# A recurrent attention with a two-layer projection on one core: the product with the state in four small tiles, more buffers for r and k, and a wait for GpSimd

## The chip, the cores and the metric

The kernel runs on one core of a Trainium2 chip. A core has TensorE (PE, matrix products; its weight loads are listed as PEld), VectorE (DVE), ScalarE (ACT), GpSimd (POOL), and SyncE (SP), which issues the DMA transfers here. They run side by side, each in the order of its own queue, and wait for each other by semaphores. The metric is the device time of one execution in microseconds; a time shown is the median of several runs.

## The reference

Inputs: `r`, `k`, `v` of shape (4, 8, 768, 48) (batch, heads, tokens, head width), a decay `w` and a bonus `u` per head and channel, and two weight matrices of 384 x 2048 and 2048 x 384 with a slope `alpha`. For each batch and head a 48 x 48 state runs over the tokens:

```python
for t in range(S):
    cur = np.einsum('bhd,bhe->bhde', u[None] * kt, vt)
    y[:, :, t] = np.einsum('bhd,bhde->bhe', rt, state + cur)
    state = w[None, :, :, None] * state + np.einsum('bhd,bhe->bhde', kt, vt)
# x = y as (3072, 384)
h = x @ w_in
g = np.maximum(h, 0.0) + alpha * np.minimum(h, 0.0)
out = g @ w_out
```

## The kernel before, in words

**Attention.** The 768 tokens are cut in six chunks of 128 (`C = 6`, `L = 128`). A unit, `attention(c, q, at)`, is one chunk `c` and one pair of heads `q` (0 to 3) for all four batches. Head 0 of the pair lies on partitions 0 to 47, head 1 on 64 to 111 (`half(g)`). With r and k scaled by powers of the decay (DVE, L302), a unit makes the scores k r in PSUM (`scores`, L342: 8 fp32 matmuls, 48 rows deep, on the two halves of the array's rows), lays them by a mask over a diagonal that holds the bonus term (ACT L349, DVE L353), and then `out` sums in the PSUM tile `y` two products: the state `T[q]` with r (L363) and v with the masked scores (L368). `state_product` makes k v (L380) into the PSUM tile `U`; DVE adds it to the decayed state (L445), one instruction for each head. An fp32 matmul is two instructions on PE, so four matmuls are eight in the trace.

`T[q]` is 112 x 4 x 112: the two heads' 48 x 48 states stand on the diagonal of each 112 x 112 block, the rest is zero (POOL memsets, L205), so one matmul of 112 rows and 112 columns serves both heads. The state of chunk 0 is copied by ACT (L440), the last chunk makes none. The bonus term of chunks 0 and 1 comes from a small matmul (L317), that of chunks 2 to 5 from POOL: r k (L327), times u (L329), then a DVE reduce (L333). `y` is split in a rounded part `xh` (ACT L410) and a rest `xl` (DVE L412), each one instruction of 112 x 512; head pair 0's rows are then copied to their places by small DMAs (`lower`).

**Projection.** A step is one chunk and one of 16 weight tiles: `m_in` (L458, 9 matmuls of 512 columns into `hp`), the activation (ACT L464, DVE L465, ACT L468, DVE L469) and, three steps later, `m_out` (L489, 9 matmuls into `acc`). 96 steps: tiles 0 to 8 for chunks 0 and 1, then tiles 9 to 15 for both, then chunks 2 to 5 with all 16. A weight tile comes by one DMA and is decoded once (`weights`: ACT L248, DVE L250, L252, L255, ACT L258 for `wh`, DVE L259 for `wl`).

**Order.** Nothing is ordered by hand. Each piece of work is handed to a planner (`Plan.add`) with its engine, an assumed duration, the buffers it reads and writes, and a rank. `in_order` simulates the engines as a list scheduler: among the pieces that are ready on an engine, the one of lowest rank goes next. The program is emitted in that order, so durations, ranks, buffer counts and dependencies all move the instructions of every engine. Buffers of one name rotate: a piece of the n-th user waits for all pieces of the (n - bufs)-th. r and k use `raw` (4 buffers); chunk 0's third pair borrows `o`, its fourth `wx`, the scratch of the weights' decode. `rr` (r for POOL) has 2 buffers, `kk` 3. In PSUM, the scores use `A0` and `A1`, `U` takes `A0` behind the scores, `y` has one bank.

Of the kernel before, what the change touches and what calls it, by code (L numbers as in the profile page):

```python
# [14 lines left out]
ALU = mybir.AluOpType  # L15
# [116 lines left out]
def rwkv_prelu_kernel(ctx: ExitStack, tc, rk, vkr, wP, uP, u, wall, alpha, w, r_all, k_all, v_all, oT):  # L132
# [41 lines left out]
    def half(h):  # L174
        return slice(HI * (h % 2), HI * (h % 2) + D)
# [100 lines left out]
    def attention(c, q, at):  # L276
        first, last = c == 0, c == C - 1

        r, k0 = (sb([112, B, L], *(("o", 2) if q == 2 else ("wx", 2)) if first and q > 1 else ("raw", 4))
                 for _ in range(2))  # L280
        v, k = sb([128, 2 * B, D], "v", 4), sb([128, 2 * B, D], "kk", 3)
        n = 2 * B * D
# [25 lines left out]
        if c < 2:  # L308
            prod = sb([112, B, L], "g", 3)
            add("DVE", 0.7, lambda: nc.vector.tensor_tensor(out=prod(), in0=r(), in1=k0(), op=ALU.mult),  # L310
                r=[r, k0], w=[prod], rank=10 * q - 88 if first else at - 3)
            sums, cols = (pb([128, 2 * B], "y"), slice(0, 8)) if c else (bank, slice(8 * q, 8 * q + 8))
            mine = sums if c else (sums, q)

            def c_sum():
                for b in range(B):
                    nc.tensor.matmul(sums()[:, cols][:, 2 * b:2 * b + 2], prod()[:, b], uw()[:, q], start=True,  # L317
                                     stop=True, skip_group_check=True)

            add("PE", 1.0, c_sum, r=[prod, uw], w=[mine], rank=at - 0.2 - 40 * first - 20 * (c == 1))  # L320
            add("ACT", 0.2, lambda: nc.scalar.activation(cu(), sums()[:, cols].rearrange("p (b g) -> p g b", g=2), AF.Copy), r=[mine],
                w=[cu], rank=at - 1)
        else:
            rt = sb([128, 2 * B, D], "rr", 2)
            load(rt, lambda: nc.sync.dma_start(rt().rearrange("p x e -> p (x e)"), vkr[c, q, :, 2 * n:]), 192,
                 early + 0.1 * q + 0.2, [wh[0]])
            add("POOL", 1.2, lambda: nc.gpsimd.tensor_tensor(out=rt(), in0=rt(), in1=k(), op=ALU.mult), r=[k], w=[rt],  # L327
                rank=at - 2)
            add("POOL", 1.2, lambda: nc.gpsimd.tensor_tensor(  # L329
                out=rt().rearrange("p (g b) e -> p g b e", g=2), in0=rt().rearrange("p (g b) e -> p g b e", g=2),  # L330
                in1=utab()[:, 2 * q:2 * q + 2, None, :].broadcast_to([128, 2, B, D]), op=ALU.mult),
                r=[utab], w=[rt], rank=at - 2)
            add("DVE", 0.55, lambda: nc.vector.tensor_reduce(  # L333
                out=cu().rearrange("p g b -> p (g b)"), in_=rt(), axis=AX.X, op=ALU.add), r=[rt], w=[cu], rank=at - 1.8)
# [20 lines left out]
                rank=10 * q - 76 + g if first else at - 1.5 if c != 1 else -60)  # L355


        y = pb([112, B, L], "y" if not first or q % 2 == 0 else "hp", 1 if not first or q % 2 == 0 else 2)

        def out():  # L360
            if not first:
                for b in range(B):
                    nc.tensor.matmul(y()[:, b], T[q]()[:, b], r()[:, b], start=(b == 0), stop=False,  # L363
                                     skip_group_check=True)
            for b in range(B):
                for g in range(2):
                    rows, x = (slice(0, HI) if first and g == 0 else half(g)), g * B + b
                    nc.tensor.matmul(y()[rows, b], v().rearrange("p x e -> p (x e)")[:, x * D:x * D + rows.stop - rows.start],  # L368
                                     base[g]()[:, b], start=first and b == 0,
                                     stop=(b == B - 1), skip_group_check=True)  # L370

        U = None

        def state_product():

            kt, vt = k().rearrange("p x e -> p (x e)"), v()
            for b in range(B):
                for g in range(2):
                    rows, x = slice(HI * g, HI if g == 0 else HI + D), g * B + b
                    nc.tensor.matmul(U()[rows, b], kt[:, x * D:x * D + rows.stop - rows.start], vt[:, x],  # L380
                                     start=(b == 0), stop=(b == B - 1), skip_group_check=True)

        def both():
# [8 lines left out]
        if not last and not first:  # L392
            U = pb([112, B, D], "A0")
# [9 lines left out]
        def split(rows, k, h, l):  # L403
            def view(t):
                return t()[rows] if k is None else t()[rows, k]

            def refs(t):
                return [t] if k is None else [(t, (k, 2))] + ([(t, (k, 0))] if rows.stop - rows.start > D else [])

            add("ACT", 0.6, lambda: nc.scalar.activation(view(h), y()[rows].rearrange("p b t -> p (b t)"), AF.Copy),  # L410
                r=[y], w=refs(h), rank=at - 1.2 if c != 1 else -60)
            add("DVE", 0.72, lambda: nc.vector.tensor_tensor(  # L412
                out=view(l), in0=y()[rows].rearrange("p b t -> p (b t)"), in1=view(h), op=ALU.subtract),
                r=[y] + refs(h), w=refs(l), rank=at - 1.2 if c != 1 else -60)

        if q == 0:
            for t, name in ((xh, "xh"), (xl, "xl")):
                t[c] = sb([128, NK, NT], name, 2, F32R)
                top[name] = sb([112, NT], name + "0", 1, F32R)
            split(slice(0, 112), None, top["xh"], top["xl"])  # L420
        elif first and q == P - 1:
            lower(c, q - 1)
            for g in range(2):
                split(half(g), q - 1, xh[c], xl[c])
        else:
            split(slice(0, 112), q - 1, xh[c], xl[c])
            lower(c, q - 1)

        def diag(g):
            return T[q]()[half(g), :, HI * g:HI * g + D]  # L430

        if first:
            def state():
                nonlocal U
                U = pb([112, B, D], "y")
                k_load()
                add("DVE", 0.56, scale_k, r=[wtok], w=[k], rank=0.5 * q - 1)
                add("PE", 0.8, state_product, r=[k, v], w=[U], rank=0.5 * q - 1)
                for g in range(2):
                    add("ACT", 0.4, lambda g=g: nc.scalar.activation(diag(g), U()[half(g)], AF.Copy), r=[U],  # L440
                        w=[(T[q], g)], rank=0.5 * q - 1)
            return state
        if not last:
            for g in range(2):
# [7 lines left out]
    def m_in(n):  # L452
        c, i = STEPS[n]
        hp = pb([128, NT], "hp", 2)
        for k in range(NK):
            def mm(k=k):
                for j, (a, x) in enumerate(((wh, xh), (wl, xh), (wh, xl))):
                    nc.tensor.matmul(hp(), a[i]()[:, k], x[c]()[:, k], start=(k == 0 and j == 0),  # L458
                                     stop=(k == NK - 1 and j == 2))

            add("PE", 0.7, mm, r=[wh[i], wl[i]] + [(t[c], (k, p)) for t in (xh, xl) for p in range(3)], w=[hp], rank=n)
# [82 lines left out]
        add("DVE", 0.1, lambda: nc.vector.tensor_copy(flag(), total()), r=[total], w=[flag], rank=at)  # L544


    begins = {}
    for n, (c, i) in enumerate(STEPS):
        begins.setdefault(c, n)
# [13 lines left out]
        jobs.append((n + MLAG - 0.5, 5, lambda n=n: m_out(n)))  # L563
    jobs.append((40, 7, check))


    def warm():
        x = ident().bitcast(mybir.dt.bfloat16)
        nc.tensor.matmul(bank()[:, 256:512], x[:, 0:128], x, start=True, stop=True, skip_group_check=True)

    add("PE", 7.0, lambda: [warm() for _ in range(33)], r=[ident], w=[(bank, "warm")], rank=-1000)
    for m in range(P):
        table(m)
    states = [attention(0, q, -50 + q) for q in range(P)]
# [148 lines left out]
```

## Time and profile before

| what | value |
|---|---|
| median of 3 runs | 536.69 us (535.27 to 537.5) |
| the profiled execution | 534.09 us |
| its span, first to last instruction | 532.4 us |
| busy | PE 516.5 us (97%), PEld 416.9, DVE 313.5 (59%), ACT 228.7 (43%), POOL 40.3 (8%) |
| chain that ended last | PE 88%, DVE 6%, DMA 2%, issue 2%, ACT 1% |
| of it, by line | L489 38%, L458 37%, L368 4%, L342 4%, L363 3%, L380 1% |
| granted clock, mean | 0.990 |
| DMA | 47.21 MB, mean 89 GB/s; 221 to 229 GB/s up to 60 us |

Times are counted in microseconds from the span's first instruction. PE's matmuls are pipelined: where one starts before the last has ended, the time between the starts is what counts, not the duration of one. A value in brackets at the end of a row of a timeline is idle time of the engine just before it, and what ended it.

### The profile page before, as it was taken

Reading aid. Unit: us, or ns where it says so; the run is one execution under the profiler, and the core shown is the slowest. Engines: PE = TensorE matmul, PEld = TensorE weight load, DVE = VectorE, ACT = ScalarE, POOL = GpSimd, SP = SyncE. Lnnn points to the kernel's source line nnn. Section 1 sums busy time; section 2 is a strip of 40 time slices with the busy share of each in tenths; the row PEclk is TensorE's granted clock in tenths of the full one; section 3 lists DMA queues with packets and bytes.
Section 4 is the critical chain, followed back from the end, with each engine's and each line's share of the span. In section 5 each row is a group of like instructions: output and inputs, shape, how many; then the busy total and the mean of one; then the engine's idle time right before and its main releaser. Section 6 shows DMA issues by size and latency. Waiting matters only on the chain.

```text
span 532.4 us, 8105 instructions
## 1 busy us (share of the span) xinstructions
PE 516.5 (97%) x3144; PEld 416.9 (78%) x3144; DVE 313.5 (59%) x481; ACT 228.7 (43%) x481; POOL 40.3 (8%) x49
## 2 busy tenths in 40 slices
PE   8999987999999999999999999999999999999994
PEld 6877766788788887888787887888877878888883
DVE  7899998998555765746653555554434333333331
ACT  4767557666443442432432542442533323332222
POOL 2000011100010211101110101121000000000000
PEclk9899998999999999999999999999999999999998
DMA  8767365442231551313220313220120000100001
GB/s 231 233 222 231 117 211 188 167 161 74 78 101 33 175 166 47 125 37 103 63 68 16 113 39 105 64 90 1 34 87 28 5 6 0 60 2 1 0 1 64
DMA packets 24877, 47.21 MB, mean 89 GB/s; under 512 B 4096, under 2 KB 12416, under 8 KB 24832
## 3 DMA queue, kind: packets, MB, share of 16 engines
q1 hardware_dynamic: 24832, 46.62, 27.5%
q8 instruction: 27, 0.44, 0.4%
q14 instruction: 18, 0.15, 0.1%
HBM read 37.96 MB, written 6.29 MB: 83 GB/s over the span
## 4 chain that ended last, share of the span: by engine, by line
PE 88%; DVE 6%; DMA 2%; issue 2%; ACT 1%; SPq 0%; DVEq 0%; ACTq 0%
PE acc L489 38%; PE hp L458 37%; PE y L368 4%; PE A L342 4%; PE y L363 3%; DMA raw<-rk 1%; PE A L380 1%; DVE wx L255 1%; DMA kk<-vkr 1%; DVE raw L302 1%; PE acc L317 1%; DVE wx L252 1%; DVE wx L250 1%; DVE xl L412 1%; DVE g L310 0%
## 5 line engine op out<-in xcount | busy, mean ns | idle before, releaser
L465 DVE SCALAR_TENSOR_TENSOR g<-hp,alph,g 128x512 f32<-128x512 f32 x96 | 72.0, 750 | 145.3 <-ACT g L464 145.2
L464 ACT ACTIVATE g<-hp 128x512 f32<-128x512 f32 x96 | 57.4, 598 | 176.3 <-PE hp L458 175.3
L458 PE MATMUL hp<-xh,wh 128*128 128x512 f32 x288 | 116.6, 405 | 0.0
L458 PE MATMUL hp<-xh,wl 128*128 128x512 f32 x288 | 114.0, 396 | 1.6 <-DVE wl L259 1.6
L458 PE MATMUL hp<-xl,wh 128*128 128x512 f32 x288 | 113.9, 396 | 0.0
L469 DVE TENSOR_TENSOR gl<-g,gh 128x512 fp32r<-128x512 f32 x96 | 67.2, 700 | 38.9 <-ACT gh L468 38.0
L468 ACT ACTIVATE gh<-g 128x512 fp32r<-128x512 f32 x96 | 60.7, 632 | 68.4 <-DVE g L465 66.4
L489 PE MATMUL acc<-gh,wh 128*128 128x512 f32 x288 | 86.0, 406 | 3.0 <-ACT gh L468 3.0
L489 PE MATMUL acc<-gh,wl 128*128 128x512 f32 x288 | 83.9, 399 | 0.0
L489 PE MATMUL acc<-gl,wh 128*128 128x512 f32 x288 | 83.1, 395 | 0.0
L489 PEld LDWEIGHTS acc<-gh,wh 128*128 128x128 f32 x288 | 52.8, 189 | 16.4 <-ACT gh L468 3.4
L458 PEld LDWEIGHTS hp<-xh,wh 128*128 128x128 f32 x288 | 54.1, 188 | 14.6 <-ACT wh L258 0.5
L458 PEld LDWEIGHTS hp<-xh,wl 128*128 128x128 f32 x288 | 54.2, 188 | 14.1 <-DVE wl L259 2.3
L489 PEld LDWEIGHTS acc<-gh,wl 128*128 128x128 f32 x288 | 54.5, 189 | 13.3
L489 PEld LDWEIGHTS acc<-gl,wh 128*128 128x128 f32 x288 | 54.4, 189 | 13.1
L458 PEld LDWEIGHTS hp<-xl,wh 128*128 128x128 f32 x288 | 54.2, 188 | 13.0
L349 ACT ACTIVATE base<-ident,cu 128x128 f32<-128x128 f32 x192 | 60.4, 390 | 0.3
L327 POOL TENSOR_TENSOR rr<-rr,kk 128x384 f32<-128x384 f32 x16 | 17.9, 1121 | 318.7 <-DMA kk<-vkr 221.6
L302 DVE TENSOR_TENSOR raw<-raw,W 112x512 f32<-112x512 f32 x44 | 34.1, 794 | 2.5 <-DMA raw<-rk 2.4
L353 DVE COPY_PREDICATED base<-strict,A 128x512 f32<-128x512 uint8 x44 | 30.2, 727 | 1.5 <-PE A L342 1.4
L342 PEld LDWEIGHTS A<-raw 48*128 48x128 f32 x336 | 20.5, 187 | 7.7 <-issue 7.7
L368 PE MATMUL y<-base,v 128*48 128x128 f32 (+1 forms) x352 | 25.5, 284 | 0.4 <-DVE base L353 0.4
(84 smaller groups left out, 375.0 us busy)
## 6 DMA issues: line engine op xcount, KB each, us to landing
wraw<-wall SPq DMA_DIRECT2D x16, 768.0 KB, 4.5
raw<-rk SPq DMA_DIRECT2D x44, 224.0 KB, 3.0
v<-vkr SPq DMA_DIRECT2D x24, 192.0 KB, 3.5
kk<-vkr SPq DMA_DIRECT2D x24, 192.0 KB, 3.3
rr<-vkr SPq DMA_DIRECT2D x16, 192.0 KB, 2.4
oT<-o SPq DMA_DIRECT2D x12, 256.0 KB, 2.2
oT<-g SPq DMA_DIRECT2D x6, 256.0 KB, 2.5
xh<-xh SPq DMA_DIRECT2D x36, 32.0 KB, 2.3
```

The lines of the kernel that those rows point to most:

```text
L302: add("DVE", 0.72, lambda t=t, tab=tab: nc.vector.tensor_tensor(out=t(), in0=t(), in1=tab().broadcast_to([112, B, L]), op=ALU.mult), r=[W[ ...
L327: add("POOL", 1.2, lambda: nc.gpsimd.tensor_tensor(out=rt(), in0=rt(), in1=k(), op=ALU.mult), r=[k], w=[rt], rank=at - 2)
L342: nc.tensor.matmul(A[g]()[:, b], k0()[half(g), b], r()[half(g), b], start=(b == 0), stop=(b == B - 1), skip_group_check=True)
L349: add("ACT", 0.36, lambda g=g, b=b: nc.scalar.activation(base[g]()[:, b], ident(), AF.Copy, scale=cu()[:, g, b:b + 1]), r=[cu, ident], w=[ ...
L353: add("DVE", 0.75, lambda g=g: nc.vector.copy_predicated(base[g](), strict()[:, None, :].broadcast_to([128, B, L]), A[g]()), r=[strict, A[ ...
L368: nc.tensor.matmul(y()[rows, b], v().rearrange("p x e -> p (x e)")[:, x * D:x * D + rows.stop - rows.start], base[g]()[:, b], start=first ...
L458: nc.tensor.matmul(hp(), a[i]()[:, k], x[c]()[:, k], start=(k == 0 and j == 0), stop=(k == NK - 1 and j == 2))
L464: add("ACT", 0.6, lambda: nc.scalar.activation(g(), hp(), AF.Copy), r=[hp], w=[g], rank=n - 100)
L465: add("DVE", 0.75, lambda: nc.vector.scalar_tensor_tensor(out=g(), in0=hp(), scalar=alph()[:, i:i + 1], in1=g(), op0=ALU.mult, op1=ALU.max ...
L468: add("ACT", 0.64, lambda: nc.scalar.activation(gh(), g(), AF.Copy), r=[g], w=[gh], rank=n - 100)
L469: add("DVE", 0.73, lambda: nc.vector.tensor_tensor(out=gl(), in0=g(), in1=gh(), op=ALU.subtract), r=[g, gh], w=[gl], rank=n - 99)
L489: nc.tensor.matmul(banks[k](), a[i]()[:, NK + k], x(), start=(begin and j == 0), stop=(end and j == 2))
```

## The change

The state `T[q]` becomes compact (112 x 4 x 48, the two heads one below the other, no zeros and no memsets). For chunks 2 to 5 the product with the state is made of eight matmuls of 48 rows and 48 columns, on the four 64x64 quarters of the array, in an order that goes round the quarters. A head's output can then land in either half of the partitions, so two PSUM tiles hold `y`, one for each head of the pair: `y[0]` in the bank `y`, where `U` takes the other columns, and `y[1]` in the bank `A1`. They are split by four ACT and four DVE instructions of 48 x 256. In chunks 0 and 1 (`plain`) one tile `y` stays; there the product with v comes first, and in chunk 1 the state's product follows in the two quarters on the diagonal. `U` is added to the state by one DVE instruction for both heads, and in chunk 0 copied by one ACT instruction. `raw` has six buffers; only chunk 0's fourth pair borrows, from `o`. In chunk 2 the first POOL product also reads weight tile 12 (`wh[12]`), so it waits for it. The warm-up matmuls are added earlier in the program's text.

```diff
-    T = [fixed([112, B, 112], f"T{m}") for m in range(P)]
+    T = [fixed([112, B, D], f"T{m}") for m in range(P)]
...
-    for m in range(P):
-        add("POOL", 0.45, lambda m=m: nc.gpsimd.memset(T[m](), 0.0), w=[T[m]], rank=-96)
...
-        r, k0 = (sb([112, B, L], *(("o", 2) if q == 2 else ("wx", 2)) if first and q > 1 else ("raw", 4))
+        r, k0 = (sb([112, B, L], *(("o", 2) if first and q == P - 1 else ("raw", 6)))
...
-            add("POOL", 1.2, lambda: nc.gpsimd.tensor_tensor(out=rt(), in0=rt(), in1=k(), op=ALU.mult), r=[k], w=[rt],
+            add("POOL", 1.2, lambda: nc.gpsimd.tensor_tensor(out=rt(), in0=rt(), in1=k(), op=ALU.mult), r=[k] + ([wh[12]] if c == 2 else []), w=[rt],
...
-        y = pb([112, B, L], "y" if not first or q % 2 == 0 else "hp", 1 if not first or q % 2 == 0 else 2)
+        U, plain = None, c < 2
+        if plain:
+            y = pb([112, B, L], "y" if not first or q % 2 == 0 else "hp", 1 if not first or q % 2 == 0 else 2)
+            if not first:
+                U = mine = pb([112, B * D], "A0")
+        else:
+            y = [pb([112, 2 * 2 * L], "y"), pb([112, 2 * L], "A1")]
+            U, mine = y[0], (y[0], "U")
+            y_of = [(y[0], "y"), y[1]]
...
         def out():
-            if not first:
+            if plain:
                 for b in range(B):
-                    nc.tensor.matmul(y()[:, b], T[q]()[:, b], r()[:, b], start=(b == 0), stop=False,
-                                     skip_group_check=True)
-            for b in range(B):
...
+                for b in () if first else range(B):
+                    for g in range(2):
+                        nc.tensor.matmul(y()[half(g), b], T[q]()[half(g), b], r()[half(g), b], start=False,
+                                         stop=(b == B - 1), skip_group_check=True)
+                return
+            for j in range(2):
+                for g, o in ((0, 0), (1, 1), (0, 1), (1, 0)):
+                    b = j + 2 * (g ^ o)
+                    nc.tensor.matmul(y[g]()[half(o), j * L:(j + 1) * L], T[q]()[half(g), b], r()[half(g), b],
+                                     start=(j == 0), stop=False, skip_group_check=True)
+            for j in range(2):
+                for g, o in ((0, 0), (1, 1), (1, 0), (0, 1)):
+                    b = j + 2 * (g ^ o)
+                    nc.tensor.matmul(y[g]()[half(o), j * L:(j + 1) * L], v()[:, g * B + b], base[g]()[:, b],
+                                     start=False, stop=(j == 1), skip_group_check=True)
...
-            add("PE", 2.0 if last else 2.6, out if last else both, r=[T[q], r, v] + base + ([] if last else [k]),
-                w=[y] + ([] if last else [U]), rank=at + 1)
+            add("PE", 1.7 if last else 2.3, out if last else both, r=[T[q], r, v] + base + ([] if last else [k]),
+                w=([y] if plain else y_of) + ([] if last else [mine]), rank=at + 1)
...
+        if not plain:
+            for g in (1, 0):
+                for o in (g, 1 - g):
+                    n0 = 0 if o == g else 2 * L
+                    split(half(g), slice(n0, n0 + 2 * L), y_of[g], half(o), kx, h, l, [2 + 2 * g + (o != g)], 0.38)
...
-            for g in range(2):
-                add("DVE", 0.42, lambda g=g: nc.vector.scalar_tensor_tensor(
-                    out=diag(g), in0=diag(g), scalar=w128()[half(g), q:q + 1], in1=U()[half(g)], op0=ALU.mult,
-                    op1=ALU.add), r=[U, (w128, q)], w=[(T[q], g)], rank=at - 1.4 if c != 1 else -61)
+            add("DVE", 0.42, lambda: nc.vector.scalar_tensor_tensor(
+                out=T[q](), in0=T[q](), scalar=w128()[:, q:q + 1], in1=u_rows(slice(0, 112)), op0=ALU.mult,
+                op1=ALU.add), r=[mine, (w128, q)], w=[T[q]], rank=at - 1.4 if c != 1 else -61)
```

## Rows read from the trace of the kernel before

**Rows 1.** Stretches: length, busy time (instructions) of each engine, granted clock, DMA share, GB/s

```profile
36.00:60.00 24.00, 22.66 (x176) 17.90 (x173) 23.66 (x38) 17.07 (x39) 0.00 (x0) 1.00 0.70 229
...
80.00:100.00 20.00, 17.03 (x98) 13.66 (x99) 18.54 (x28) 12.89 (x29) 4.63 (x4) 0.91 0.57 182
100.00:144.00 44.00, 44.00 (x190) 35.46 (x189) 36.87 (x54) 27.36 (x48) 0.00 (x0) 1.00 0.29 101
```

**Rows 2.** Timeline of PE, 308 to 318 us: start, length, engine, line, tiles, shape, instructions

```profile
308.96 0.39 PE L458 MATMUL hp<-xl,wh 128*128 128x512 f32 x1
309.28 1.16 PE L342 MATMUL A<-raw 48*128 48x128 f32 x16
...
314.44 0.40 PE L458 MATMUL hp<-xl,wh 128*128 128x512 f32 x1
314.68 1.04 PE L363 MATMUL y<-raw,T 112*112 112x128 f32 x8
315.65 1.08 PE L368 MATMUL y<-base,v 128*48 128x128 f32 x16
316.56 0.61 PE L380 MATMUL A<-v,kk 128*64 128x48 f32 x16
```

**Rows 3.** The chain that ended last, same place: start, length, what

```profile
309.35 1.09 PE A L342 x16
310.44 2.30 PE acc L489 x9
312.74 2.10 PE hp L458 x9
314.84 0.88 PE y L363 x8
```

**Rows 4.** Timelines of POOL and ACT, and a piece of the chain, 72 to 146 us

```profile
72.39 1.01 POOL L327 TENSOR_TENSOR rr<-rr,kk 128x384 f32<-128x384 f32 x1 [67.97 <-DMA kk<-vkr]
...
81.23 1.02 POOL L327 TENSOR_TENSOR rr<-rr,kk 128x384 f32<-128x384 f32 x1 [6.15 <-DMA kk<-vkr]
...
113.29 0.85 ACT L258 ACTIVATE wh<-wx 128x768 fp32r<-128x768 f32 x1 [0.23 <-DVE wx L255]
...
144.51 1.09 PE A L342 x16
```

**Rows 5.** Timeline of DVE, 66 to 85 us, five of its instructions

```profile
66.97 0.55 DVE L250 TENSOR_SCALAR wx<-wx 128x768 uint32<-128x768 uint32 x1
67.56 0.96 DVE L252 SCALAR_TENSOR_TENSOR wx<-wraw,wx 128x768 uint32<-128x768 uint32 x1
...
72.61 1.61 DVE L255 SCALAR_TENSOR_TENSOR wx<-wraw,wx 128x768 uint32<-128x768 uint32 x1
...
81.51 1.16 DVE L250 TENSOR_SCALAR wx<-wx 128x768 uint32<-128x768 uint32 x1
82.70 1.63 DVE L252 SCALAR_TENSOR_TENSOR wx<-wraw,wx 128x768 uint32<-128x768 uint32 x1
```

**Rows 6.** Timeline of PE, 71 to 86 us, and its chain from 85.72

```profile
71.19 1.04 PE L363 MATMUL y<-raw,T 112*112 112x128 f32 x8
...
72.77 0.96 PE L368 MATMUL y<-base,v 128*48 128x128 f32 x13 [0.20 <-DVE base L353]
...
77.03 0.50 PE L458 MATMUL hp<-xh,wl 128*128 128x512 f32 x1 [1.39 <-DVE wl L259]
...
85.72 1.65 PE L489 MATMUL acc<-gh,wh 128*128 128x512 f32 x3 [2.97 <-ACT gh L468]
...
85.72 3.70 PE acc L489 x9
```

**Rows 7.** Groups by line and shape: busy us, mean ns, idle before

```profile
L445 DVE SCALAR_TENSOR_TENSOR T<-T,w,A 48x192 f32<-48x192 f32 x32 | 13.2, 411 | 9.6 <-PE A L380 9.4
...
L410 ACT ACTIVATE xh<-y 112x512 fp32r<-112x512 f32 x22 | 13.0, 590 | 17.7 <-PE y L368 17.7
...
L333 DVE TENSOR_REDUCE cu<-rr 128x8 f32<-128x384 f32 x16 | 8.7, 544 | 0.3 <-POOL rr L329 0.3
```

More of the change, by code (lines that the diff above doesn't have):

```diff
@@ L360, in out, with u_rows @@
+        def u_rows(rows):
+            return U()[rows].rearrange("p (b e) -> p b e", b=B) if plain else \
+                U()[rows, 2 * L:2 * L + B * D].rearrange("p (b e) -> p b e", b=B)
         def out():
-            if not first:
+            if plain:
                 for b in range(B):
-                    nc.tensor.matmul(y()[:, b], T[q]()[:, b], r()[:, b], start=(b == 0), stop=False,
-                                     skip_group_check=True)
-            for b in range(B):
-                for g in range(2):
[L367 to L370, printed above, removed]
@@ L372, in attention @@
-        U = None
+                    for g in range(2):
+                        rows, x = (slice(0, HI) if g == 0 else half(g)), g * B + b
+                        nc.tensor.matmul(y()[rows, b], v().rearrange("p x e -> p (x e)")[
+                            :, x * D:x * D + rows.stop - rows.start], base[g]()[:, b], start=b == 0,
+                            stop=first and b == B - 1, skip_group_check=True)
+                for b in () if first else range(B):
+                    for g in range(2):
+                        nc.tensor.matmul(y()[half(g), b], T[q]()[half(g), b], r()[half(g), b], start=False,
+                                         stop=(b == B - 1), skip_group_check=True)
@@ L379, in state_product @@
                     rows, x = slice(HI * g, HI if g == 0 else HI + D), g * B + b
-                    nc.tensor.matmul(U()[rows, b], kt[:, x * D:x * D + rows.stop - rows.start], vt[:, x],
+                    nc.tensor.matmul(u_rows(rows)[:, b], kt[:, x * D:x * D + rows.stop - rows.start], vt[:, x],
                                      start=(b == 0), stop=(b == B - 1), skip_group_check=True)
@@ L390, in scale_k @@
                                     in1=wtok()[:, 2 * q:2 * q + 2, None, :].broadcast_to([128, 2, B, D]))
-        if not last and not first:
-            U = pb([112, B, D], "A0")
         if first:
@@ L398, in attention, with split, psum @@
                 add("DVE", 0.56, scale_k, r=[wtok], w=[k], rank=at - 1.6)
-            add("PE", 2.0 if last else 2.6, out if last else both, r=[T[q], r, v] + base + ([] if last else [k]),
-                w=[y] + ([] if last else [U]), rank=at + 1)
-        def split(rows, k, h, l):
+            add("PE", 1.7 if last else 2.3, out if last else both, r=[T[q], r, v] + base + ([] if last else [k]),
+                w=([y] if plain else y_of) + ([] if last else [mine]), rank=at + 1)
+        def split(out_rows, cols, src, rows, k, h, l, parts, us):
             def view(t):
-                return t()[rows] if k is None else t()[rows, k]
+                return t()[out_rows, cols] if k is None else t()[out_rows, k, cols]
             def refs(t):
[L408 to L414, printed above, removed]
+                return [(t, (k, p)) for p in parts]
+            def psum():
+                t = src[0] if isinstance(src, tuple) else src
+                return t()[rows].rearrange("p b t -> p (b t)") if plain else t()[rows, 0:2 * L]
+            at_x = at - 1.2 if c != 1 else -60
+            add("ACT", us, lambda: nc.scalar.activation(view(h), psum(), AF.Copy), r=[src], w=refs(h), rank=at_x)
+            add("DVE", us + 0.1, lambda: nc.vector.tensor_tensor(out=view(l), in0=psum(), in1=view(h),
+                                                                 op=ALU.subtract),
+                r=[src] + refs(h), w=refs(l), rank=at_x)
         if q == 0:
@@ L459, in mm @@
                                      stop=(k == NK - 1 and j == 2))
-            add("PE", 0.7, mm, r=[wh[i], wl[i]] + [(t[c], (k, p)) for t in (xh, xl) for p in range(3)], w=[hp], rank=n)
+            add("PE", 0.7, mm, r=[wh[i], wl[i]] + [(t[c], (k, p)) for t in (xh, xl) for p in range(6)], w=[hp], rank=n)
         g = sb([128, NT], "g", 3)
@@ L544, in check, with warm @@
         add("DVE", 0.1, lambda: nc.vector.tensor_copy(flag(), total()), r=[total], w=[flag], rank=at)
+    def warm():
+        x = ident().bitcast(mybir.dt.bfloat16)
+        nc.tensor.matmul(bank()[:, 256:512], x[:, 0:128], x, start=True, stop=True, skip_group_check=True)
+    add("PE", 7.0, lambda: [warm() for _ in range(33)], r=[ident], w=[(bank, "warm")], rank=-1000)
     begins = {}
@@ L564, in rwkv_prelu_kernel @@
     jobs.append((40, 7, check))
[L567 to L571, printed above, removed]
     for m in range(P):
```

23 lines of the change are left out of this document (10 added, 13 removed).

## The prediction

> **What bounds the kernel now.** I read the page first (the table above): TensorE (PE) is busy 97% of the span and the chain that ended last lies 88% on it. An average hides stages, so next comes the view of stretches [rows 1]. From 100 us on PE is busy for all of a stretch (44.00 of 44.00 us), while VectorE (DVE) has 7 us to spare. Before 100 us it is the other way: DVE is full (23.66 of 24.00 us from 36 to 60, 18.54 of 20.00 from 80 to 100) and PE has holes (17.03 of 20.00 between 80 and 100 us, where the granted clock falls to 0.91). So there are two regimes. After about 92 us each microsecond taken off PE's own work is a microsecond of the end, and what is put on DVE or ScalarE (ACT) is hidden; before that, DVE's order sets the time, and PE's stalls are what can be won.
>
> Third, the price of the product with the state, from PE's timeline in an undisturbed place [rows 2] and the chain there [rows 3]. The state product (L363) is 8 instructions (four fp32 matmuls, two instructions each), 128 moving columns each, in 0.88 us, or 0.11 us apiece. The product with v (L368) is 16 instructions with the same 128 columns, started from 315.65 to 316.56: 0.91 us. Twice the instructions in the same time, because its two heads write to two halves of the array's columns: two tiles run at once, a pair every 0.11 us. The scores (L342), tiled by rows, show the same: 16 in 1.09 us. A change of tile shape shows too: the plain matmul at 308.96 is followed by the scores 0.32 us later, the one at 314.44 by the (untiled) state product 0.24 us later, so 0.08 us is lost on entry; from L363 to L368 it is 0.97 - 0.88 = 0.09 us; back in the plain shape nine matmuls take 2.30 instead of 2.10 us.
>
> **State product in 64x64 tiles, 16 units (chunks 2 to 5, four head pairs each).** It removes 8 instructions of 0.11 us and adds 16 on four tiles, four on each. The trace has no four tiles at once. From below: all four together, four rounds, 4 x 0.11 = 0.44 us. From above: only pairs, as in both tiled rows of [rows 2], 8 x 0.11 = 0.87 us; or one by one, 16 x 0.11 = 1.76 us. I take 0.44: row halves run side by side (L342), column halves run side by side (L368), and in L380 two tiles have unequal work and yet 16 instructions of 48 columns go through in 0.54 us, so neither tile nor the issue of instructions holds the other up at 0.034 us apiece; 16 instructions in 0.44 us are 0.027 apiece. New is the change of shape on entry: 0.08 us, and in the first round 0.04 (L368: 0.91 against 8 x 0.109 = 0.87) to 0.10 us. The 0.09 us to L368 stays. New: 0.44 + 0.08 + 0.07 = 0.59 against 0.88 us; 0.29 us saved, **16 x 0.29 = 4.6 us**, all on the path.
>
> What hangs on it: y now lies in two banks and is split in four parts. ACT and DVE each read 48x256 four times in place of 112x512 once (590 ns on ACT [rows 7]). No row has this shape; the nearest is the 48x192 state update (411 ns), so 0.4 us each, between 0.3 (half of 590) and 0.59 (no shorter). That adds about 1.0 us on each of the two per unit; one state update of 112x192 in place of two of 48x192 gives 0.4 back on DVE. PE covers it: in 100 to 144 us DVE has 7 us idle while it still decodes weights, and afterwards it has less to do. Without that cover, 1.6 us per unit (1.0 and 1.0 - 0.4), or 26 us, would be at stake, but a split is first read several steps of 4.2 us (hp and acc, 2.10 each) after its product. The second half of y takes a bank that the scores use, and the state product leaves the other; the next scores are a pair of steps later, so I put this at nothing.
>
> **Chunk 1 (plain path).** The product with v now goes first, in column halves, and the state product follows in two diagonal tiles: 16 instructions in pairs, 0.87 against 0.88 us. Two more changes of shape cost about 0.25 us a unit, 1.0 us in all. The new order has another price: at 71.19 PE does the state product first and then waits 0.20 us for the mask (DVE L353) [rows 6]; with v first it stands for the 0.97 us before (314.68 to 315.65 in [rows 2]). This happens in two units of four, the first and the third. Both costs fall where PE would wait for DVE anyway.
>
> **Chunk 2's r k u held until weight tile 12.** This is the edit with the largest lever. GpSimd (POOL) works on chunk 2 at 72.39 and 81.23 us [rows 4], and the DVE instructions beside it stretch: L255 to 1.61 and L250 to 1.16 us, L252 to 1.63, against 0.55 and 0.96 undisturbed [rows 5]. (L255 is L252's shape.) Straight after come PE's two largest stalls: 1.39 us for wl at 77.03 and 2.97 us for gh at 85.72, and then nine matmuls take 3.70 instead of 2.10 us because the clock fell [rows 6]. Weight tile 12 is written at 113.29 us; chunk 2's first scores run at 144.51 [rows 4], so the held work (two pairs at once, some 2.3 us each, then DVE's reduce and ACT's 8 diagonals) still has over 20 us. Queued behind it on POOL is only its own kind. SP's load of the third r buffer waits for the reduce of the first, and moves with it. The collisions move to a stretch where PE waits for no DVE.
>
> The sum: at 77.03 the stall of 1.39 goes, but the later start of 0.97 us at 71.19 eats most: 0.4. At 85.72 gh waits for DVE's turn at the activation, which stands in its queue behind the two stretched instructions: these give 1.28 us back (0.61 + 0.67), and chunk 2's reduce (0.54 us [rows 7]) and k scaling (the same 384 columns; 0.4 is my estimate) leave the queue ahead of it, so the stall falls from 2.97 to 0.8: 2.15. The clock then holds: 1.6. Less 0.5 us for half of chunk 1's extra changes of shape: 0.4 + 2.15 + 1.6 - 0.5 = **3.6 us**. Bounds: 6.0 us (both stalls and the clock, all) and -2.9 us (nothing won, 1.0 + 2 x 0.97 paid).
>
> **Six buffers for r and k; the compact state.** Chunk 1's third pair is loaded earlier, chunk 0's last pair leaves the weights' scratch buffers. Costed at nothing: between 36 and 60 us DVE is full, and what arrives sooner waits for it; if the pair's two loads (112x512 fp32 each, 0.46 MB at the 229 GB/s of [rows 1], 2 us) came in front of a weight tile in SP's queue they would cost up to that, and if they left such a place, gain it. The four POOL memsets of the state go (POOL is idle there), and chunk 0 saves four short ACT copies. The move of the warm-up matmuls in the text puts nothing in another place.
>
> **The sum.** 4.6 + 3.6 = 8.2 us. The profiled execution took 534.09 us (span 532.4 and 1.7 around it): 525.9. The median of the runs shown is 2.6 higher; there it is 536.69 - 8.2 = **528.5 us**.
>
> **Rivals.**
> 1. The early gain doesn't come: the planner writes another order, or another wait steps in (gh for the same accumulation is late by ACT and DVE alone; weights by their loads). For it: DVE is full from 36 to 100 us, so a stall removed can come back as the next. Against: the two stalls stand right behind the stretched instructions. Only the tiles: 536.69 - 4.6 = 532.1.
> 2. Chunk 1's two diagonal tiles don't run at once, because they lie in different rows of the array and write one bank: 16 x 0.11 = 1.76 against 0.88 us, 4 x 0.87 = 3.5 us. The scores, the only row-tiled matmuls here, write two banks, so no row speaks for or against. 528.5 + 3.5 = 532.0, less what a stall hides. The Trainium skill has such a rule (TensorEngine Tiling (Array Packing), section Restrictions and Gotchas): different row tiles can't access the same PSUM bank simultaneously. By that rule chunk 1 pays and chunks 2 to 5, with their two banks, don't.
> 3. Four tiles run as pairs only: 0.87 + 0.12 = 0.99 against 0.88 us, 16 x 0.11 = 1.8 us lost; with the early 3.6, 534.9. For it: no row here shows more than two. Against: the independence of the halves both ways.
> 4. The slower side: the four tiles of the state product go one by one, 1.76 + 0.12 = 1.88 us, 1.0 us lost in each of 16 units: 536.69 + 16 - 3.6 = 549.1. It decides from a state product of 0.88 + 3.6/16 = 1.1 us. Against: both tiled rows of [rows 2].
>
> **How the numbers follow.** Forecast 0.58 (its own range 525 to 531.5), rival 1 0.17, rival 2 0.08, rival 3 0.10, rival 4 0.04, and 0.03 for none of them. The predicted time is the forecast's. Low end: 6.0 early and 5.8 from the tiles (nothing lost on entry beyond the 0.08) are 11.8, which gives 524.9; with a little for the scatter of three runs, 524.5. High end: rivals 1 and 2 are inside, 3 and 4 (0.14) are not: 534.0. Half a per cent is 2.7 us, about what a measurement of this kernel can tell: faster than 534.0 takes the first three cases less their upper edge, 0.81; rival 3 is the middle, 0.13; the rest slower, 0.06.
>
> **What would show it.** The chain in chunks 2 to 5: a state product of 16 instructions in about 0.5 us, 0.6 with its entry, and 0.9 us for v as before. Between 60 and 100 us: DVE L250 at 0.55 and L252 at 0.96 throughout, POOL's first tensor work after 110 us, PE's stalls under 1 us each and the clock at 1.0. In chunk 1: no more than 0.9 us for the diagonal tiles, and a longer wait for L353. DVE and ACT each some 8 to 15 us busier. The prediction is wrong if PE has holes after 100 us, if the state product stays near 0.9 us, or if a stall of 2 us or more is left before 92 us.

## The result and the profile after

The changed kernel takes 527.69 us in the median of four runs (526.22 to 530.25), the kernel before 535.98 us beside it (532.0 to 537.5). The ratio is 0.9875, its 95% interval 0.9829 to 0.992: faster by 6.7 us (4.3 to 9.2); the two medians lie 8.3 apart. The forecast of 528.5 us and its range held, but one of its two halves came out by other routes than the text gave.

The profiled execution is the slowest of the four: 530.25 us. The page, first lines and the chain by engine:

```profile
span 528.5 us, 8481 instructions
...
PE 515.8 (98%) x3310; PEld 409.3 (77%) x3310; DVE 322.5 (61%) x513; ACT 242.5 (46%) x525; POOL 41.3 (8%) x45
...
PE 94%; DVE 2%; ACT 2%; issue 1%; DMA 1%; SPq 0%; ACTq 0%
```

The share of PE on the chain rose from 88 to 94%: the path lies on TensorE more than before. The view of stretches, columns as in [rows 1]:

```profile
36.00:60.00 24.00, 22.17 (x186) 16.46 (x184) 22.62 (x38) 14.98 (x34) 0.00 (x0) 1.00 0.68 216
60.00:80.00 20.00, 18.33 (x150) 14.35 (x151) 15.70 (x25) 10.64 (x22) 2.59 (x2) 0.83 0.46 148
80.00:100.00 20.00, 19.96 (x146) 15.45 (x145) 18.12 (x27) 11.05 (x22) 3.22 (x3) 1.00 0.60 192
100.00:144.00 44.00, 44.00 (x190) 35.44 (x189) 40.61 (x59) 28.86 (x54) 2.86 (x2) 1.00 0.35 118
144.00:250.00 106.00, 106.00 (x752) 83.83 (x754) 68.63 (x113) 49.59 (x116) 14.00 (x12) 1.00 0.34 105
```

PE's holes between 80 and 100 us have gone (17.03 to 19.96 us busy). Instead the stretch from 60 to 80 us has a low clock, 0.83, and POOL works in both (2.59 and 3.22 us), where the prediction had it idle. From 100 us on PE has no hole, as before. PE's timeline at the first four-tile state product (L386), start and length first:

```profile
153.20 0.31 PE L386 MATMUL y<-raw,T 48*48 48x128 f32 x1
153.21 0.31 PE L386 MATMUL A<-raw,T 48*48 48x128 f32 x1
153.21 0.31 PE L386 MATMUL y<-raw,T 48*48 48x128 f32 x1
153.22 0.31 PE L386 MATMUL A<-raw,T 48*48 48x128 f32 x1
153.35 0.27 PE L386 MATMUL y<-raw,T 48*48 48x128 f32 x1
...
153.46 0.27 PE L386 MATMUL y<-raw,T 48*48 48x128 f32 x1
...
153.56 0.27 PE L386 MATMUL y<-raw,T 48*48 48x128 f32 x1
...
153.78 0.31 PE L391 MATMUL y<-base,v 128*48 128x128 f32 x1
```

Four matmuls start within 0.02 us, two into each of y's two tiles (the second lies in the bank A1 and is shown as A); the next fours follow at 153.35, 153.46 and 153.56, 0.11 us apart (0.15 to the second). From 153.20 to the product with v at 153.78 it is 0.58 us, for 0.97 us (314.68 to 315.65) in [rows 2].

Two steps in the chains of waits, first of before, then of after (start, length, what), say what that came to:

```profile
138.21 2.10 PE hp L458 x9
...
516.96 2.10 PE hp L458 x9
```

```profile
140.67 2.10 PE hp L481 x9
...
513.41 2.10 PE hp L481 x9
```

The first row of each is one and the same step, the second the last step. After is 2.46 us behind at the first and 3.55 ahead at the last. Of the 2.46, 1.29 are only order: chunk 2's first scores and the change of shape behind them (1.09 and 0.20 us), which stand at 144.51 in [rows 4], run at 95.21 in after. So this execution lost 1.17 us early and won 3.55 + 1.17 = 4.72 us behind it, 0.295 for each of 16 units.

The early loss has more than one source. The first projection step starts at 33.97 us for 31.62, so after is 2.35 us behind there already. Part of that goes with the clock, 0.83 up to 20 us for 0.91 in before. A second execution of after (After again, below) has 0.91 there too and still starts its first step at 33.20. The next loss comes in chunk 1. PE's timeline and POOL's, after, 51 to 86 us (in brackets the wait ahead and what ended it):

```profile
51.73 1.08 PE L380 MATMUL y<-raw,T 48*48 48x128 f32 x16
52.74 0.67 PE L400 MATMUL A<-v,kk 128*64 128x48 f32 x16
...
61.39 1.07 PE L375 MATMUL y<-base,v 128*48 128x128 f32 x14 [1.52 <-DVE base L350]
62.39 1.95 PE L380 MATMUL y<-raw,T 48*48 48x128 f32 x16
```

```profile
77.33 1.82 POOL L324 TENSOR_TENSOR rr<-rr,kk 128x384 f32<-128x384 f32 x1 [73.74 <-DMA kk<-vkr]
...
84.68 1.02 POOL L324 TENSOR_TENSOR rr<-rr,kk 128x384 f32<-128x384 f32 x1 [4.44 <-DMA kk<-vkr]
```

Chunk 1's two diagonal tiles take 1.01 us at the full clock (51.73 to 52.74). In the second of chunk 1's four units PE stands 1.52 us for the mask (L350). In before the second unit has no such wait; 0.18 us stands in the first and the 0.20 of [rows 6] in the third. After the wait of 1.52 us the two diagonal tiles take 1.95 us for 1.08, at a granted clock of 0.83 in the stretch. And POOL starts chunk 2's products at 77 and 85 us, released by a DMA and not by weight tile 12: the tie to wh[12] is no wait on the chip, other than the section on the change says. The instruction reads no byte of that tile, and what the tie does is to change the order that the planner writes.

**Time against clock.** One kernel's runs scatter by 2 to 8 us, and most of it goes with the mean granted clock. Over the 152 runs compared, of all kernels, I fitted time = base of the kernel + slope x (1 - mean clock), one slope for all and one base for all runs of before: 464 (17 either way) us, and 0.77 us of scatter is left. One run of 998.31 us, of the kernel without the tie and at a full clock, stands far from all others and is left out. The bases compare kernels at an equal clock, more finely than medians; they are an estimate. They leave out what an edit does to the clock itself, for instance by taking away a stall and the low clock behind it. After is 5.8 (0.4) us below before in its first set and 5.4 (0.3) in a second; its mean clock is 0.9897 for 0.9869, which is 464 x 0.0028 = 1.3 us more.

### The profile page after: what moved, and what is told of

It reads as the page before. It is cut to its first block, busy times and chain, and to the rows that moved or that the text cites. A ratio compares the mean times of both kernels' runs of the same rounds, so it can differ in the third digit from the quotient of the medians.

```text
span 528.5 us, 8481 instructions
## 1 busy us (share of the span) xinstructions
PE 515.8 (98%) x3310; PEld 409.3 (77%) x3310; DVE 322.5 (61%) x513; ACT 242.5 (46%) x525; POOL 41.3 (8%) x45
## 4 chain that ended last, share of the span: by engine, by line
PE 94%; DVE 2%; ACT 2%; issue 1%; DMA 1%; SPq 0%; ACTq 0%
PE hp L481 38%; PE acc L512 38%; PE A L339 5%; PE y L391 2%; PE y L386 2%; PE y L375 1%; PE A L391 1%; PE y L400 1%; PE y L380 1%; PE acc L314 1%; PE acc L572 1%; PE y L314 1%; ACT base L346 1%; DMA raw<-rk 1%; PE A L400 1%
## 5 line engine op out<-in xcount | busy, mean ns | idle before, releaser
L324 POOL TENSOR_TENSOR rr<-rr,kk 128x384 f32<-128x384 f32 x16 | 20.5, 1282 | 314.6 <-DMA kk<-vkr 218.7
L299 DVE TENSOR_TENSOR raw<-raw,W 112x512 f32<-112x512 f32 x46 | 36.3, 809 | 0.6 <-DMA raw<-rk 0.6
L350 DVE COPY_PREDICATED base<-strict,A 128x512 f32<-128x512 uint8 x44 | 30.5, 729 | 2.7 <-PE A L339 2.4
L339 PEld LDWEIGHTS A<-raw 48*128 48x128 f32 x352 | 23.0, 197 | 8.2 <-issue 7.1
L339 PE MATMUL A<-raw 48*128 48x128 f32 x352 | 27.5, 296 | 0.3 <-DVE wtok L224 0.3
```

Of the source, the lines that this page charges most:

```text
L299: add("DVE", 0.72, lambda t=t, tab=tab: nc.vector.tensor_tensor(out=t(), in0=t(), in1=tab().broadcast_to([112, B, L]), op=ALU.mult), r=[W[ ...
L339: nc.tensor.matmul(A[g]()[:, b], k0()[half(g), b], r()[half(g), b], start=(b == 0), stop=(b == B - 1), skip_group_check=True)
L350: add("DVE", 0.75, lambda g=g: nc.vector.copy_predicated(base[g](), strict()[:, None, :].broadcast_to([128, B, L]), A[g]()), r=[strict, A[ ...
```

## The experiments

I held after the traces: the tiles bring 4.7 us; the tie only reorders; what the early part brings or costs comes from the order, the buffers and chunk 1's v-first. The rival was the prediction's own account, that POOL's work beside DVE is the price. Three sets, each with before on its chip. "At equal clock" is the difference from before by the fit. With a base of before for each set (529.0, 528.8 and 529.4 us), the differences of the second set, from After again on, would be 0.2 us smaller, those of the third, from Before with the tie alone on, 0.4 larger.

**Tiles alone**: four buffers and the borrowed ones as before, no tie.

```
-        r, k0 = (sb([112, B, L], *(("o", 2) if first and q == P - 1 else ("raw", 6)))
+        r, k0 = (sb([112, B, L], *(("o", 2) if q == 2 else ("wx", 2)) if first and q > 1 else ("raw", 4))
...
-  ... r=[k] + ([wh[12]] if c == 2 else []), w=[rt],
+  ... r=[k], w=[rt],
```

> The tile change alone: the changed kernel with r and k buffered as before (four buffers, o and wx borrowed) and without the tie to weight tile 12. Theory A (from the trace of after: the tiles give 16 x 0.29 = 4.7 us in chunks 2 to 5, everything before 100 us only reshuffles): 4 to 6 us below before, ratio about 0.991, all of it in steps after 150 us. Rival R (the forecast's other half, the removed collisions, gave the rest): the same 4.6 us here, since R's part is left out; what would tell against both is a state product that gives nothing without the other two edits.

531.16 us, ratio 0.9916 (0.9883 to 0.9948); 3.8 (0.3) less at equal clock. The tiles carry most, though less than 4.7. Chunk 2's first state product in before:

```profile
151.93 1.04 PE L363 MATMUL y<-raw,T 112*112 112x128 f32 x8
```

From there to the last step it is 365.03 us in before (to 516.96), 360.21 in after (153.20 to 513.41) and 360.17 here. So the tiles' price is whole here, and the missing 0.9 was lost ahead of chunk 2.

**No tie**: after, with the second half of that edit.

> The changed kernel without the tie of chunk 2's POOL product to weight tile 12. Theory A: POOL starts at the same time as with it, about 77 us, because the tie is only known to the planner and no semaphore stands on POOL; all that differs is that DVE does chunk 2's first reduce and k scaling (0.55 us each) early, so 0 to 1.5 us slower than the changed kernel. Rival R (the tie keeps POOL off DVE): POOL moves by 30 us and the time is about 3.6 us more, 531 to 532.

530.39 us (529.99 without the one long run), 0.9908 (0.9873 to 0.9944); 4.9 (0.3) less at equal clock, with a mean clock of 0.9873 for after's 0.9897. The tie's part of the result is under a microsecond and hardly apart from nothing (5.4 to 5.8 with it).

**Four buffers**: after, with the first half.

> The changed kernel with r and k buffered as before. Theory A: the third pair's load no longer stands in SP's queue before the first weight tiles waiting for chunk 0's scores (in the changed kernel the two weight loads are issued at 18.1 us, before at 14.7), the first step starts at about 31.6 instead of 34.0 us, and the kernel is 1 to 2.5 us faster than the changed one, if DVE keeps up. Rival R (buffers cost and give nothing): the same within 0.7 us.

531.13 us, 0.993 (0.9899 to 0.9961); 3.4 (0.3) less at equal clock, so the six buffers, which I had costed at nothing, are worth 2.0 to 2.4 us beside the tie (3.4 for after's 5.4 and 5.8) and 1.1 without it (4.9 - 3.8). My guess that they cost something by delaying the first weights fell: with four buffers the first step starts as late (33.86 us, for 34.0 with six and 31.6 before). What else in the change delays it was not taken apart.

**A real wait**: after, and a small POOL product that reads weight tile 12 goes ahead of chunk 2's first.

```
+    scrap = fixed([128, 8], "scrap")
...
+            if c == 2 and q == 0:
+                def hold():
+                    x = wh[12]()[:, 0, 0:8].bitcast(F32)
+                    nc.gpsimd.tensor_tensor(out=scrap(), in0=x, in1=x, op=ALU.mult)
+
+                add("POOL", 0.2, hold, r=[wh[12]], w=[scrap], rank=at - 2)
...
-  ... r=[k] + ([wh[12]] if c == 2 else []), w=[rt],
+  ... r=[k] + ([wh[12], scrap] if c == 2 else []), w=[rt],
```

> The changed kernel, with one small POOL instruction that reads weight tile 12 ahead of chunk 2's products, so that POOL really waits until about 115 us. Theory A: DVE was hardly stretched in the changed kernel's order (1.10 for 0.95 us at 79.95, 0.83 for 0.69 at 85.42, some 0.3 us in all), so within 1 us of the changed kernel. Rival R (collisions of POOL with DVE cost PE its stalls): 2 to 4 us faster than the changed kernel, 524 to 526.

POOL's timeline shows the hold that the prediction meant:

```profile
115.89 0.91 POOL L328 TENSOR_TENSOR scrap<-wh 128x8 f32<-128x8 f32 x1 [112.31 <-ACT wh L256]
116.76 1.32 POOL L331 TENSOR_TENSOR rr<-rr,kk 128x384 f32<-128x384 f32 x1
```

527.46 us, 0.9872 (0.9838 to 0.9906); 5.8 (0.3) less at equal clock: no more than after has. In after's order POOL's work lies where PE doesn't stand behind it. PE's wait for the mask is there as well (1.50 us), with a clock of 1.00 from 60 to 80 us behind it.

**After again**, unchanged, for the second set.

> The changed kernel itself once more, as the base of this set. Theory B (from the first set: all executions of a kernel lie on one line, time = base + 467 us x (1 - granted clock), and the bases are 529.0 before, 525.1 with the tiles alone, 523.2 with the whole change): 526 to 529.5, ratio 0.985 to 0.989, and 523.2 on that line at clock 1.

528.45 us, 0.9884 (0.9844 to 0.9923). The wait for the mask is there again, 1.51 us at 60.64, and the clock falls to 0.91 in that stretch. So the wait belongs to the order, while the low clock behind it comes in some executions only: none in the kernel with the real wait, nor in the doubled one below (1.51 us, clock 1.00).

**State first in chunk 1**: the two diagonal tiles go before v, so that PE has work while DVE masks. Each T is padded by 16 zeroed columns, so that the first tile can start all the rows of y.

```
...
+            if c == 1:
+                for b in range(B):
+                    for g in range(2):
+                        rows = slice(0, HI) if g == 0 else half(g)
+                        nc.tensor.matmul(y()[rows, b], state(half(g), b, rows.stop - rows.start), r()[half(g), b],
+                                         start=b == 0, stop=False, skip_group_check=True)
+                for b in range(B):
+                    for g in range(2):
+                        nc.tensor.matmul(y()[half(g), b], v()[:, g * B + b], base[g]()[:, b], start=False,
+                                         stop=b == B - 1, skip_group_check=True)
+                return
...
```

> The changed kernel, with chunk 1's product with the state put ahead of the product with v again, still in two diagonal tiles. Theory B: PE's 1.5 us wait for the mask of the second unit (61.39 us) shrinks by the 1.0 us of the state product, and the clock falls less often behind it: base 0.5 to 1 us lower, mean 1 to 2 us lower than the changed kernel. Rival: DVE and ACT set the time there, PE's order is hidden; within 0.5 us.

PE's timeline, second unit:

```profile
61.23 1.08 PE L381 MATMUL y<-raw,T 48*64 48x128 f32 x16
62.25 0.42 PE L385 MATMUL y<-base,v 128*48 128x128 f32 x2
63.41 0.97 PE L385 MATMUL y<-base,v 128*48 128x128 f32 x13 [0.74 <-DVE base L353]
```

The wait is 0.74 for 1.51 us, and the stretch from 60 to 80 us keeps a clock of 1.00. 525.07 us, 0.9809 (0.9766 to 0.9853); 7.4 (0.35) less at equal clock. This beats both kernels: 3.4 us under after, 1.9 (0.45) of it at equal clock, the rest with the clock (0.9923 for 0.9893, 1.4 us). Of the 1.9, 0.77 is the shorter wait. Up to another 0.6 goes with the order of the shapes: an undisturbed unit of chunk 1 takes 2.47 us (74.42 to 76.89) for after's 2.62 (76.28 to 78.90) and before's 2.42 (89.26 to 91.68), 0.15 less in each of four. The last half microsecond is about the error.

**Two tiles in all chunks**: the same two diagonal tiles from chunk 2 on.

```
-        U, plain = None, c < 2
+        U, plain = None, True
```

> The changed kernel with the plain path in all chunks: one y, the state product in two diagonal tiles, in chunks 2 to 5 too. Theory: eight rounds of 0.11 us instead of four and one more change of shape, 0.44 + 0.15 to 0.2 a unit, 16 units: 9 to 10.5 us slower than the changed kernel, 536.5 to 538.5, so no faster than before. If the gain came from the order and not from four tiles at once: within 2 us of the changed kernel.

537.5 us, 1.0041 (1.0004 to 1.0078): slower than before. Its chain, one unit:

```profile
152.09 1.02 PE y L375 x15
153.10 1.01 PE y L380 x16
154.11 0.60 PE A L400 x14
154.71 2.29 PE hp L481 x9
```

152.09 to 154.71 is 2.62 us; after's chain takes 2.04 there (153.27 to 155.31):

```profile
153.27 0.24 PE y L386
...
155.31 0.43 PE hp L481
```

16 x 0.58 = 9.3 us, and 9.0 is what the medians of the set show (537.5 - 528.45), 8.7 the fit. The tiles' price follows from the row.

**Product twice**: after, each four-tile state product issued twice (the state's share partly counts twice).

```
-            for j in range(2):
+            for j in (0, 1, 0, 1):
```

> The changed kernel with the state product of chunks 2 to 5 issued twice (part of the state's share of y is then counted twice), the planner told nothing. Theory: four more rounds of 0.109 us with no further change of shape, 16 x 0.44 = 7.0 us more than the changed kernel, all of it after 150 us. If the four tiles went as pairs it would be 14 us, if the path were hidden by DVE or ACT under 2 us.

534.63 us, 0.9987 (0.9953 to 1.002); 6.2 us over after again in the medians and 7.2 at equal clock. Four more rounds of 0.11 us in 16 units are 7.0, and from chunk 2's first state product to the last step the trace has 367.21 us for 360.22 in after again: 7.0. So four rounds cost what four rounds of one tile cost, and all of it lies on the path.

**Before with the tie alone.**

```
-  ... r=[k], w=[rt],
+  ... r=[k] + ([wh[12]] if c == 2 else []), w=[rt],
```

> The kernel before, with nothing changed but the tie of chunk 2's POOL product to weight tile 12, which only the planner sees. Theory C (POOL still starts at 72 and 81 us, only DVE's reduce and k scaling move): within 1 us of before. Forecast's theory R (the edit itself removes the collisions): 3.6 us faster, minus the 0.4 us that belongs to the product order, ratio 0.994.

530.27 us, 0.9909 (0.9876 to 0.9941), but only 1.5 (0.35) less at equal clock; its mean clock was 0.9935. PE's, POOL's and DVE's timelines:

```profile
74.59 0.50 PE L458 MATMUL hp<-xh,wl 128*128 128x512 f32 x1 [1.39 <-DVE wl L259]
...
81.03 0.96 PE L489 MATMUL acc<-gh,wh 128*128 128x512 f32 x3 [0.74 <-ACT gh L468]
```

```profile
69.95 1.01 POOL L327 TENSOR_TENSOR rr<-rr,kk 128x384 f32<-128x384 f32 x1 [65.45 <-DMA kk<-vkr]
71.04 1.61 POOL L329 TENSOR_TENSOR rr<-rr,utab 128x384 f32<-128x384 f32 x1
```

```profile
70.04 1.73 DVE L255 SCALAR_TENSOR_TENSOR wx<-wraw,wx 128x768 uint32<-128x768 uint32 x1
71.70 1.50 DVE L469 TENSOR_TENSOR gl<-g,gh 128x512 fp32r<-128x512 f32 x1
```

The order alone takes the larger stall from 2.97 [rows 6] to 0.74 us; the collision at 70 us and the stall of 1.39 behind it stay. POOL works from 78.62 us here too, but this time its own instruction is the long one (1.76 us), and L250 and L252 take 0.55 and 0.95.

**Before with the real wait.** The tie and the small product, on before.

> The kernel before, with the tie and a small POOL instruction that reads weight tile 12, so that POOL really starts after 113 us. Theory R (POOL stretches DVE's L255, L250, L252 at 72 to 84 us and PE's stalls of 1.39 and 2.97 us follow from that): 3 to 5 us faster than before, ratio 0.991 to 0.994, with no stall over 1 us left between 70 and 90 us. Theory C (the stalls come from DVE's load alone, as e4 suggests): within 1 us of e9.

PE's timeline and DVE's at the same places:

```profile
75.17 0.50 PE L465 MATMUL hp<-xh,wl 128*128 128x512 f32 x1 [0.23 <-DVE wl L260]
...
81.62 0.96 PE L496 MATMUL acc<-gh,wh 128*128 128x512 f32 x3 [0.74 <-ACT gh L475]
```

```profile
72.23 0.95 DVE L256 SCALAR_TENSOR_TENSOR wx<-wraw,wx 128x768 uint32<-128x768 uint32 x1
73.09 0.69 DVE L476 TENSOR_TENSOR gl<-g,gh 128x512 fp32r<-128x512 f32 x1
```

With POOL away the two DVE instructions fall to 0.95 and 0.69 us, the first stall from 1.39 to 0.23, the second to 0.74 (forecast: 0.8). 527.92 us, 0.9866 (0.9829 to 0.9904); 3.9 (0.35) less at equal clock. In the median one wait on the kernel before does as much as the whole change (8.0 us under its set's before; after's two sets have 8.3 and 7.0); at equal clock it does two thirds (3.9 for 5.4 to 5.8), the rest goes with its mean clock of 0.9923.

**Four buffers with the real wait.** The four-buffer kernel, plus the wait.

> The changed kernel with four buffers for r and k, the tie, and the real POOL wait. In e3 (the same without the wait) POOL ran at 81 to 88 us beside DVE's gl (1.48), L249 (1.63) and L252 (1.65 us), and the mask that PE waited 2.05 us for came behind them. Theory R: 1.5 to 3 us faster than e3, 528 to 529.5, so level with the changed kernel; six buffers then help only by shifting POOL's work to a harmless place. Theory C: level with e3, 531.

529.23 us, 0.9855 (0.9821 to 0.9889); 5.55 (0.3) less at equal clock, 2.1 more than without the wait. PE's timeline in the kernel without it and with it:

```profile
91.06 1.58 PE L375 MATMUL y<-base,v 128*64 128x128 f32 x16 [2.05 <-DVE base L350]
```

```profile
90.35 1.07 PE L382 MATMUL y<-base,v 128*48 128x128 f32 x14 [0.26 <-DVE base L357]
```

So six buffers and the real wait buy much the same 2 us: each gets POOL's work out of the way of a mask.

**State first with the real wait.**

> e6 (state product first in chunk 1) with the real POOL wait: the candidate for the fastest. If collisions still cost in e6's order (POOL at 72 to 84 us there): 1 us below e6, 524. If not: e6's 525 within 1 us. Against before: ratio 0.977 to 0.982.

525.93 us, 0.9812 (0.9786 to 0.9838); 7.4 (0.3) less at equal clock, where the state-first kernel alone has 7.4. The wait adds nothing there that these runs can tell.

## Why the prediction was right, and where its reasons failed

- **Tiles, 4.6 us: right, in mechanism and size.** 4.72 in the traces, and the two-tile and the doubled kernel show the same price from both sides (9.0 or 8.7 for 9.3, 7.0 or 7.2 for 7.0). The stretch from chunk 2's first state product to the last step is 360.2 to 360.3 us in all nine traces of a kernel with the four tiles as they are, and 365.0 in all three with the old product, whatever the order ahead of it. Forecast for the unit's state product 0.59 us, measured 0.58 (153.27 to 153.85 in the chain). Rivals 3 (pairs only) and 4 (one by one) are out.
- **Their cost on ACT and DVE: hidden, as said.** By the groups, after:

```profile
L434 DVE TENSOR_TENSOR xl<-A,xh 48x256 fp32r<-48x256 f32 x32 | 13.5, 422 | 4.1 <-ACT xh L433 3.3
...
L433 ACT ACTIVATE xh<-y 48x256 fp32r<-48x256 f32 x32 | 12.2, 380 | 3.2 <-DVE T L468 2.3
```

0.42 and 0.38 us for the estimate of 0.4; DVE is 9.0 and ACT 13.8 us busier (forecast 8 to 15), and PE has no hole from 144 to 250 us (106.00 of 106.00).
- **Rival 2: out.** Chunk 1's diagonal tiles write one bank and take 1.01 us for 16 instructions with the change of shape (forecast 0.87), not 1.76. The rule that the Trainium skill gives (TensorEngine Tiling (Array Packing), section Restrictions and Gotchas), that different row tiles can't access one PSUM bank at once, isn't borne out here for tiles that differ in rows and columns.
- **Rival 1: true in part.** Another order was written and another wait stepped in, the 1.52 us for the mask; a part of the early gain came all the same.
- **Held r k u: the step that failed.** "The collisions move to a stretch where PE waits for no DVE" took the tie for a wait. POOL's first tensor work came at 77.33 us, not after 110. On the kernel before, a real wait does what the forecast said of it. For the first stall the mechanism is shown: with the tie alone it stays at 1.39 us, with POOL away it is 0.23. The second falls to 0.74 with the tie alone as well, so what stretched instructions and what DVE's queue each had in it is not shown. The forecast's terms for the two stalls, without the price of chunk 1's new order, which this kernel doesn't have, are 1.39 + 2.15 = 3.5 us, and 1.6 for the clock; measured are 3.9 at equal clock and 2.5 with the clock (0.9923 for 0.9869). In after the large stalls went by another way: with six buffers and the tie the planner's order puts POOL's work beside harmless DVE instructions. PE's waits from 60 to 110 us, by what ended them (total us, times, longest):

```profile
PE y L375 <- DVE base L350: 1.5, 1, 1.5
PE acc L512 <- ACT gh L491: 0.3, 1, 0.3
```

- **Chunk 1's v-first: the second failed step.** "Both costs fall where PE would wait for DVE anyway" did not hold: the state product had been PE's work while DVE masked, and without it PE waits 1.52 us. The wait stands in the second unit and not, as forecast, in the first and the third; with four buffers the long one (2.05 us) stands in the fourth. The two changes of shape cost 0.20 us in an undisturbed unit (2.62 for 2.42), forecast 0.25. State first gives back 1.9 us at equal clock, and 3.4 in the median.
- **Six buffers, at nothing: mis-sized.** 1.1 to 2.4 us, put down to the order here, since a real wait with four buffers gives as much.
- **The sum.** Forecast 4.6 + 3.6 = 8.2; measured 6.7 (4.3 to 9.2), or 8.3 between the medians. By the fit the first set gives 5.8 at equal clock and 1.3 with the clock: the early part beside the tiles is about 1.1 + 1.3 = 2.4 (2.0 by the ratio) for 3.6, of which 1.6 were to be the clock's. The right time rests on the tiles; the early half is right in sign, by offsetting errors, and that it came as near as it did is luck. Of the 3.9 that a real wait is worth on before, after has about 1, and v-first explains 1.9, with its changes of shape in it; the remaining microsecond was not taken apart. A candidate is the first step, which starts at 33.20 and 33.45 us in the two traces of the changed family with a clock of 0.91 up to 20 us, and at 31.62 and 31.26 in the two of before's.
- **Open.** Why the clock falls in some executions of a kernel and not in others (one of 530.25 us at 0.985, one of 526.22 at 0.993) was not settled. The traces show where: after 100 us it is 1.00 in all of them, from 60 to 100 us between 0.83 and 1.00, and up to 20 us, ahead of most of what the edits move, between 0.77 and 1.00 (0.97 to 1.00 from 20 to 36).

## What to carry to other kernels

A dependency between instructions that share no data orders a plan but holds nothing on the chip: look for the semaphore in the trace before you count on the wait. On a path that one engine fills, an instruction's price read from one undisturbed row multiplies out to within some 6%; where several engines take turns, single effects don't add (real wait 3.9 and tiles 3.8 at equal clock, together with four buffers 5.55), so price the order that results and not the edit. And work that needs no late operand goes first: it is the cover of the wait that follows.

## What the runs showed of the hardware

- **POOL and DVE take turns.** In the rows of before with the tie, DVE's L255 starts at 70.04 and takes 1.73 us; POOL's first product ends at 70.96. 1.73 less these 0.92 us leaves 0.81, near the undisturbed 0.95. POOL's second starts at 71.04 and ends 0.88 us after L255 (71.77), for 1.01 alone; gl starts at 71.70 and ends 0.55 us after POOL (72.65), for 0.69. So the later one stands for nearly all of the other's instruction, and which is stretched depends on who came first: in after DVE's L299 starts at 77.13, and POOL's from 77.33 is the long one (1.82 us). The Trainium skill says (SBUF — State Buffer, section Who interferes with whom) that a DVE instruction with two SBUF inputs contends with a GpSimd instruction that reads SBUF, as these do; the trace agrees. That the later one blocks fully it says of DVE's two-port modes, and these rows come near it.
- **Time and clock.** One line, 464 us per unit of mean clock, holds for all kernels of the study to 0.77 us. It shows what a median alone hides: the kernel with the tie alone is 4.6 us under before in the mean, but 3.1 of that (464 x 0.0066) come with its clock of 0.9935, and 1.5 at an equal clock. Whether the plan had a part in the clock the fit can't say: in the trace the clock is 1.00 from 80 to 100 us, where before has 0.91 behind its stall of 2.97, but also 1.00 for 0.91 up to 20 us.
